# Halving the first two blocks of the first token tile, and a new order of the front, in a gated linear attention with a feed-forward network

## The chip, the cores and the metric

The kernel runs on one core of a Trainium2 chip. The metric is device microseconds of one execution. The engines are TensorE (PE, with its weight loads shown apart as PEld), VectorE (DVE), ScalarE (ACT), GpSimd (POOL) and SyncE (SP), which here only issues transfers.

## The reference

An mLSTM attention over 4 sequences, 8 heads, 768 steps and head size 40 gives `y`. The 3072 tokens of 320 features then go through a feed-forward layer of 2048 hidden features:

```python
C = f_stab * C + i_stab * outer(vt, kt)          # per head, 40 x 40
n = f_stab * n + i_stab * kt
y[t] = sigmoid(o_gate[t]) * (C @ qt) / max(|n . qt|, 1)

h = x @ w_in
g = where(h >= 1, h, where(h <= -1, 0, (h + 1)**2 / 4))
out = g @ w_out
```

All inputs and the output are float32.

## The kernel before

**Attention.** The 768 steps are cut into 6 chunks of 128, so that there are 24 units `n` (chunk `n // 4`, sequence `n % 4`), each of 8 heads by 128 steps. For a unit, `score.n` multiplies keys by queries on PE and the decay matrix `A` onto that on DVE; `main.n` multiplies with the values on PE (`up`), adds the carried state from chunk 1 on, divides on DVE and POOL (`z`, `y`, with the sigmoid of the output gates `sig`), transposes the result on PE, copies its high part to `xh` on ACT and writes the low part to `xl` on DVE. `carry.n` makes the state for the next chunk.

**Feed-forward.** A tile `j` of 512 tokens is four units, `X[j] = (xh, xl)`. The hidden features are 16 blocks of 128 columns; block number `x` is `16 * j + fc`. `mm.x` (function `mm1`, line 833) is eight PE matmuls of 512 columns into one PSUM bank; `relu.x` is two ACT instructions, `max.x` one DVE instruction. The second product comes in two forms. `out.x` takes the float32 result `r` and the float32 weights `of`: eight matmul records a block. The split form makes a high part (`gh.x`, ACT) and a low part (`gl.x`, DVE), and multiplies with split weights `oh`, `ol`: `outh.x` and `outl.x`, twelve matmuls a block. Before, blocks 0 to 9 use `out`, blocks 10 to 95 the split form. The split weights of block pair `i` are made by `so.i` (one ACT, one DVE instruction).

**Weights.** `W.k` loads a packed part of the weights: even `k` is 256 columns of `w_in` (768 KB), odd `k` 256 rows of `w_out` (640 KB). `w.k` steps convert it. For an even `k` they are, in order: `mg` and `lo` on ACT, `and` and `or` on DVE, `wh` on ACT, `wl` on DVE. An odd `k` has the first four. All of it lies beside the attention of chunks 0 and 1 and the first tile.

**Gates of the first chunk.** `fi.0` loads them, `sums.0` runs their scans on DVE, `mask` and `add` build the exponents of a sequence on PE, and `dec` takes the exponential on ACT. `bmax`, `bsum`, `btail` do the same scans for chunks 1 to 4 at once; between the first two, SP sends the running maxima through memory (`m_b`, four small transfers). `og.c` loads the output gates of chunk `c` (640 KB), `sig.c` takes their sigmoid on ACT. `hot.k` are `k` matmuls of zeros, which do no work.

**Order.** The order of everything is written out by hand in the string `STEPS` (lines 48 to 161). `InOrder` (line 174) makes each engine run its instructions in that order, SP its transfers too. So an instruction that waits holds up all that follow it on its engine. Up to eight transfers of SP's queue are under way at a time.

The steps around the change, as they are before: `og.0` is the 21st transfer of SP, `W.0` the fourth; `mm.0` comes after all four `main.n` of chunk 0 have been transposed, since `mm1` needs all 512 tokens of `X[0]`:

```python
    def load_og(c):
        t = sig[c] = ld.tile([P, B, DM], F32, name="sig", bufs=1)
        nc.sync.dma_start(t.rearrange("p b e -> p (b e)"), og[c, :, :B * DM])
```

Of the kernel before, what the change touches and what calls it, by code (L numbers as in the profile page):

```python
# [19 lines left out]
L = 128  # L20
NC = S // L
DM = H * D
# [179 lines left out]
def mlstm_ffn_kernel(ctx, tc, qk, qs, qn, vk, og, fi0, fi, fib, w_in, w_out, cst, out):  # L202
# [362 lines left out]
    def load_og(c):  # L565
        t = sig[c] = ld.tile([P, B, DM], F32, name="sig", bufs=1)
        nc.sync.dma_start(t.rearrange("p b e -> p (b e)"), og[c, :, :B * DM])

    def sigmoid(c):
        nc.scalar.activation(sig[c], sig[c], AF.Sigmoid)  # L570
# [292 lines left out]
    def mm2(x, g, part, ts=range(NTC)):  # L863
        j, fc = divmod(x, NFC)
        if j not in ops:
            ops[j] = [psum_a() for _ in range(NTC)]
# [165 lines left out]
```

## Time and profile before

| | us |
|---|---|
| median of 3 runs | 467.97 (467.7 to 468.16) |
| the profiled execution | 469.77 |
| its span, first to last instruction | 467.8 |
| PE busy | 459.0 (98%) |
| DVE busy | 353.6 (76%) |
| ACT busy | 326.0 (70%) |
| POOL busy | 145.2 (31%) |

The span is what the trace shows; 1.97 us of the profiled execution lie outside it. In the timeline, PE matmuls overlap one another, so what one costs is the distance from its start to the start of the next, and a row with `xN` merges N of them.

### The profile page before, as it was taken

Reading aid. Unit: us, or ns where it says so; the run is one execution under the profiler, and the core shown is the slowest. Engines: PE = TensorE matmul, PEld = TensorE weight load, DVE = VectorE, ACT = ScalarE, POOL = GpSimd, SP = SyncE. Lnnn points to the kernel's source line nnn. Section 1 sums busy time; section 2 is a strip of 40 time slices with the busy share of each in tenths; the row PEclk is TensorE's granted clock in tenths of the full one; section 3 lists DMA queues with packets and bytes.
Section 4 is the critical chain, followed back from the end, with each engine's and each line's share of the span. In section 5 each row is a group of like instructions: output and inputs, shape, how many; then the busy total and the mean of one; then the engine's idle time right before and its main releaser. Section 6 shows DMA issues by size and latency. Waiting matters only on the chain.

```text
span 467.8 us, 8748 instructions
## 1 busy us (share of the span) xinstructions
PE 459.0 (98%) x3312; PEld 407.8 (87%) x3312; DVE 353.6 (76%) x635; ACT 326.0 (70%) x587; POOL 145.2 (31%) x153
## 2 busy tenths in 40 slices
PE   6999999999999999999999999999999999999997
PEld 3788787888989999989999989989989898889896
DVE  5686879689999899998988889877876676243443
ACT  3659889989887677858576878757768564555562
POOL 2364123132353454542334445253113232000000
PEclk9899999999999999999999999999999999999999
DMA  6898956916084445564337353362482000000001
GB/s 204 287 299 275 351 142 227 349 45 168 28 232 121 110 139 156 141 179 112 104 106 196 80 170 90 71 189 53 118 240 80 2 0 1 2 28 29 0 1 56
DMA packets 23048, 60.60 MB, mean 130 GB/s; under 512 B 2599, under 2 KB 9535, under 8 KB 23007
## 3 DMA queue, kind: packets, MB, share of 16 engines
q1 hardware_dynamic: 22719, 59.81, 43.0%
q8 instruction: 26, 0.43, 0.4%
q10 hardware_dynamic: 288, 0.25, 0.2%
q14 instruction: 15, 0.12, 0.1%
HBM read 55.96 MB, written 4.01 MB: 128 GB/s over the span
## 4 chain that ended last, share of the span: by engine, by line
PE 96%; DMA 1%; SPq 1%; issue 1%; ACT 0%; DVE 0%; DVEq 0%
PE ps L188 96%; DMA raw<-in_qk 1%; SPq L188 1%; ACT mg L188 0%; ACT xh L188 0%; DVE z L188 0%; ACT r L188 0%; SPq L185 0%; DVE y L188 0%; DVEq L188 0%; DVE ow L188 0%
## 5 line engine op out<-in xcount | busy, mean ns | idle before, releaser
L188 PE MATMUL ps<-oh,gh 128*128 128x320 f32 x344 | 104.7, 314 | 0.0
L188 PE MATMUL ps<-ow,gh 128*128 128x320 f32 x344 | 102.9, 309 | 0.0
L188 PE MATMUL ps<-xh,wh 128*128 128x512 f32 x288 | 101.4, 406 | 0.9 <-ACT xh L188 0.9
L188 PE MATMUL ps<-xh,wl 128*128 128x512 f32 x288 | 98.2, 395 | 0.0
L188 ACT ACTIVATE r<-ps,half 128x512 f32<-128x512 f32 x96 | 65.4, 682 | 44.3 <-PE ps L188 38.1
L188 DVE SCALAR_TENSOR_TENSOR r<-ps,r 128x512 f32<-128x512 f32 x96 | 64.9, 686 | 35.1 <-ACT r L188 34.8
L188 DVE TENSOR_TENSOR gl<-r,gh 128x512 fp32r<-128x512 f32 x86 | 65.6, 772 | 22.3 <-ACT gh L188 21.4
L188 ACT CAST gh<-r 128x512 fp32r<-128x512 f32 x86 | 52.5, 615 | 40.7 <-PE ps L188 25.9
L188 PEld LDWEIGHTS ps<-ow,gh 128*128 128x128 f32 x344 | 64.7, 188 | 1.4
L188 PEld LDWEIGHTS ps<-oh,gh 128*128 128x128 f32 x344 | 64.6, 188 | 1.4
L188 PE MATMUL ps<-oh,gl 128*128 128x320 f32 x344 | 65.6, 311 | 0.0
L188 PEld LDWEIGHTS ps<-xh,wl 128*128 128x128 f32 x288 | 54.0, 188 | 12.9
L188 ACT ACTIVATE r<-r 128x512 f32<-128x512 f32 x96 | 60.7, 633 | 3.0
L188 PE MATMUL ps<-xl,wh 128*128 128x512 f32 x192 | 60.3, 395 | 0.0
L188 PEld LDWEIGHTS ps<-xh,wh 128*128 128x128 f32 x288 | 50.3, 188 | 8.7 <-ACT xh L188 1.1
L188 PEld LDWEIGHTS ps<-oh,gl 128*128 128x128 f32 x344 | 54.3, 188 | 1.1
L188 ACT ACTIVATE Abc<-Abc,nA 128x128 f32<-128x128 f32 x160 | 50.1, 392 | 3.6 <-POOL Abc L188 3.5
L188 POOL TENSOR_TENSOR v<-vk,G 128x328 f32<-128x328 f32 x36 | 29.1, 811 | 67.5 <-issue 26.2
L188 POOL TENSOR_TENSOR m<-m 128x1024 bf16<-128x1024 f32 x16 | 32.1, 2009 | 48.1 <-DVE m L188 43.0
L188 PEld LDWEIGHTS ps<-xl,wh 128*128 128x128 f32 x192 | 36.0, 188 | 8.8
L188 DVE SCALAR_TENSOR_TENSOR stk<-raw,ident,qs 120x1024 fp32r<-120x1024 f32 x28 | 39.3, 1405 | 4.8 <-ACT raw L188 4.8
L188 POOL TENSOR_TENSOR y<-y,z 128x320 f32<-128x320 f32 x24 | 20.0, 834 | 68.9 <-DVE y L188 68.9
(145 smaller groups left out, 699.2 us busy)
## 6 DMA issues: line engine op xcount, KB each, us to landing
qs<-in_qs SPq DMA_DIRECT2D x28, 480.0 KB
Abc<-a_d SPq DMA_DIRECT2D x20, 512.0 KB
vk<-in_vk SPq DMA_DIRECT2D x20, 324.0 KB
wraw<-in_w_in SPq DMA_DIRECT2D x8, 768.0 KB
wraw<-in_w_out SPq DMA_DIRECT2D x8, 640.0 KB
sig<-in_og SPq DMA_DIRECT2D x6, 640.0 KB
qn<-in_qn SPq DMA_DIRECT2D x20, 180.0 KB
raw<-in_qk SPq DMA_DIRECT2D x20, 160.0 KB
```

The source lines that it names most:

```text
L188: r = getattr(self.engine, name)(*args, **kwargs)
```

## The change

Four things are changed, all of them in how the work is cut and ordered; what is computed is the same.

1. The first two blocks of the first tile (`fc` 0 and 1 of tile 0) are made in two halves of 256 tokens. `am.fc.h` is `mm1` for half `h` alone (eight matmuls of 256 columns), `ar` and `ax` are its `relu` and `max`, `ao` its second product for two of the four token groups. The results lie in tiles of the pool `ow`.
2. `X[j]` is laid out by halves: `[half][k][256]` in place of `[k][512]`. A whole block's matmul now reads its 512 columns in two runs of 256.
3. The output gates of chunk 0 come in two transfers of 320 KB (`og.0.0`, `og.0.1`), with a sigmoid for each (`sig.0.0`, `sig.0.1`).
4. `STEPS` is new from start to end. Blocks 6 to 9 take the split form (four `gh`, four `gl` and their `outh` and `outl` in place of `out.6` to `out.9`). The other steps are the same in number, in another order. The `hot` matmuls are 20 before and 20 after.

The new front, cut after the first use of the second product:

```
fi.0 mask.0 og.0.0 id.0 sums.0 hot.4 sig.0.0 add.0 dec.0.0 dec.0.1 fb.0 bmax.0 hot.2 mask.2 add.2 mask.1
add.1 dec.1.0 gtail.0 gex.0 qk.0 score.0 score.0 score.0 qk.1 score.1 score.1 vv.0 one.0 v1.0 dec.1.1
vv.2 bmax.0 bsum.0 bsum.0 dec.2.0 dec.2.1 v1.2 W.0 mask.3 w.0 w.0 main.0 qk.3 W.1 v1.1 score.1 main.1
add.3 dec.3.1 dec.3.0 hot.2 hot.2 bsum.0 btail.0 btail.0 btail.0 score.3 main.0 main.0 w.0 hot.2 hot.2
hot.2 hot.2 main.1 hot.2 w.0 w.0 main.1 w.1 w.1 btail.0 main.1 score.3 score.3 qk.2 w.0 main.0 main.0
exps.0 score.2 main.0 v.1 v2.1 carry.1 main.1 v.0 v2.0 score.2 score.2 v1.3 main.2 og.0.1 main.1 sig.0.1
w.1 main.3 v.4 am.0.0 w.1 main.2 main.2 main.2 main.3 decs.0 main.2 main.3 main.3 W.2 carry.0 v2.4 w.2
main.2 main.3 main.3 decs.0 w.2 w.2 w.2 cs.0 A.6 prep.6 prep.6 carry.1 am.1.0 carry.0 am.0.1 ar.0.0
ax.0.0 ar.0.1 ax.0.1 am.1.1 qn.5 w.2 w.2 v.5 v2.5 carry.4 main.5 -- ar.1.0 ax.1.0 qn.4 main.4 carry.5
carry.5 carry.5 ao.0.0 ...
```

The diff of the code:

```diff
+    def load_og(c, part=None):
+        if not part:
+            sig[c] = ld.tile([P, B, DM], F32, name="sig", bufs=1)
+        bs = slice(0, B) if part is None else slice(2 * part, 2 * part + 2)
+        nc.sync.dma_start(sig[c][:, bs].rearrange("p b e -> p (b e)"), og[c, :, bs.start * DM:bs.stop * DM])
...
+    def halves(x):
+        return x.rearrange("p k t -> p (k t)").rearrange("p (h k t) -> p h k t", h=2, t=TT // 2)
...
-        xh, xl = X[j]
-        cs = slice(r * L, (r + 1) * L)
+        xh, xl = (halves(x)[:, r // 2] for x in X[j])
+        cs = slice(r % 2 * L, (r % 2 + 1) * L)
...
-    def mm1(j, fc):
-        xh, xl = X[j]
+    def mm1(j, fc, hs=slice(0, 2)):
+        xh, xl = (halves(x)[:, hs] for x in X[j])
...
-        hp = psum_a()[:, :TT]
+        hp = psum_a()[:, :(hs.stop - hs.start) * TT // 2]
...
-            nc.tensor.matmul(hp, w[:, wi, fs], x[:, xi, :], start=(i == 0), stop=(i == len(prod) - 1))
+            nc.tensor.matmul(hp, w[:, wi, fs], x[:, :, xi, :], start=(i == 0), stop=(i == len(prod) - 1))
...
+    def scratch(x, hh):
+        if x not in early:
+            early[x] = ow.tile([P, 656], F32, name="ow")
+        return early[x][:, hh * TT // 2:(hh + 1) * TT // 2]
...
+        if kind == "am":
+            block[n, ns[1]] = mm1(0, n, slice(ns[1], ns[1] + 1))
+        elif kind == "ar":
+            gs[n, ns[1]] = relu(block[n, ns[1]], scratch(*ns))
+        elif kind == "ax":
+            largest(block[n, ns[1]], gs[n, ns[1]])
+        elif kind == "ao":
+            mm2(n, gs[n, ns[1]], "r", range(2 * ns[1], 2 * ns[1] + 2), 2 * ns[1])
```

## Rows read from the trace of the kernel before

**Rows 1.** The page, sections 1 and 2: PE, and PE's granted clock in 40 slices.

```profile
PE 459.0 (98%) x3312; PEld 407.8 (87%) x3312; DVE 353.6 (76%) x635; ACT 326.0 (70%) x587; POOL 145.2 (31%) x153
...
PEclk9899999999999999999999999999999999999999
```

**Rows 2.** The chain that ended last: start us, us, what.

```profile
34.55 338.67 PE ps L188 x2487
...
373.22 91.13 PE ps L188 x588
```

**Rows 3.** Busy time by stretch: us, then PE, PEld, DVE, ACT, POOL, PEclk, DMA.

```profile
0.00:34.55 34.55, 29.24 (x237) 22.11 (x238) 23.62 (x70) 17.35 (x28) 14.08 (x29) 0.95 0.85 263
34.55:118.00 83.45, 83.45 (x492) 69.54 (x493) 68.16 (x119) 75.08 (x136) 25.18 (x26) 1.00 0.68 220
```

**Rows 4.** The timeline of PE, 0 to 35 us: start us, us, operation, idle before.

```profile
2.56 1.49 PE L188 MATMUL ps<-late_t,idb 128*128 128x512 bf16 x3
3.84 1.06 PE L188 MATMUL ps<-zeros 128*128 128x512 bf16 x2
...
5.57 0.39 PE L188 MATMUL ps<-ac,pick 96*128 96x128 bf16 x4 [0.18 <-DVE ac L188]
...
6.45 0.59 PE L188 MATMUL ps<-zeros 128*128 128x512 bf16 x2
...
19.47 2.06 PE L188 MATMUL ps<-raw 40*128 40x128 f32 x32
21.46 1.04 PE L188 MATMUL ps<-zeros 128*128 128x512 bf16 x4
...
24.91 1.88 PE L188 MATMUL ps<-ow,Abc 128*128 128x41 f32 x16
...
29.52 0.85 PE L188 MATMUL ps<-ident,y 128*128 128x128 f32 x6
...
31.83 0.87 PE L188 MATMUL ps<-ow 128*120 128x123 f32 x6
```

**Rows 5.** The timeline of PE at a block, two unsplit second products and a split one.

```profile
36.52 0.63 PE L188 MATMUL ps<-xh,wh 128*128 128x512 f32 x2
...
38.38 0.79 PE L188 MATMUL ps<-C,qn 120*128 120x123 f32 x6
...
71.80 4.47 PE L188 MATMUL ps<-ow,r 128*128 128x320 f32 x16
76.11 0.80 PE L188 MATMUL ps<-C,qn 120*128 120x123 f32 x6
...
404.10 0.75 PE L188 MATMUL ps<-oh,gl 128*128 128x320 f32 x4
...
405.85 0.75 PE L188 MATMUL ps<-oh,gl 128*128 128x320 f32 x4
```

**Rows 6.** The timeline of DVE, 11 to 36 us.

```profile
15.49 0.62 DVE L188 TENSOR_TENSOR fi_b<-fi_b,m_b 128x128 f32<-128x128 f32 x2 [2.22 <-DMA m_b<-m_r]
...
16.66 0.42 DVE L188 TENSOR_TENSOR_SCAN fi_r<-rst,fi_r 128x128 f32<-128x128 f32 x1
...
18.05 1.28 DVE L188 TENSOR_TENSOR Abc<-ps,Abc 128x512 f32<-128x512 f32 x2
```

**Rows 7.** The timeline of ACT: the first weights landed, and the first block's activation.

```profile
7.37 0.89 ACT L185 ACTIVATE mg<-wraw 128x768 f32<-128x768 f32 x1 [5.36 <-DMA wraw<-in_w_in]
8.17 1.05 ACT L188 ACTIVATE win<-wraw 128x768 uint16<-128x768 uint16 x1
...
37.73 0.70 ACT L188 ACTIVATE r<-ps,half 128x512 f32<-128x512 f32 x1
```

**Rows 8.** Groups of ACT over the whole run: count, busy us, mean ns, idle before.

```profile
L188 ACT CAST gh<-r 128x512 fp32r<-128x512 f32 x86 | 52.5, 615 | 40.7 <-PE ps L188 25.9 <-DVE r L188 14.6
```

**Rows 9.** What ACT waited for, 34.55 to 118 us: total, times, longest.

```profile
ACT mg L188 <- DVE ow L188: 2.2, 3, 1.3
...
ACT wh L188 <- DVE win L188: 1.8, 1, 1.8
```

More of the change, by code (lines that the diff above doesn't have):

```diff
@@ L563, in row, with sigmoid @@
         return n % B * NC + n // B
[L565 to L570, printed above, removed]
+    def load_og(c, part=None):
[3 more added lines that the diff above has]
+        nc.sync.dma_start(sig[c][:, bs].rearrange("p b e -> p (b e)"), og[c, :, bs.start * DM:bs.stop * DM])
+    def sigmoid(c, part=None):
+        x = sig[c] if part is None else sig[c][:, 2 * part:2 * part + 2]
+        nc.scalar.activation(x, x, AF.Sigmoid)
     def load_qk(n):
@@ L809, in main @@
         j, r = divmod(n, NTC)
-        if r == 0:
+        if j not in X:
             X[j] = (xs.tile([P, 3, TT], F32R, name="xh"), xs.tile([P, 2, TT], F32R, name="xl"))
-        xh, xl = X[j]
-        cs = slice(r * L, (r + 1) * L)
+        xh, xl = (halves(x)[:, r // 2] for x in X[j])
+        cs = slice(r % 2 * L, (r % 2 + 1) * L)
         xv = xp[:, :3 * P].rearrange("p (k t) -> p k t", t=L)
@@ L839, in mm1, with relu @@
         for i, (w, wi, x, xi) in enumerate(prod):
-            nc.tensor.matmul(hp, w[:, wi, fs], x[:, xi, :], start=(i == 0), stop=(i == len(prod) - 1))
+            nc.tensor.matmul(hp, w[:, wi, fs], x[:, :, xi, :], start=(i == 0), stop=(i == len(prod) - 1))
         return hp
-    def relu(hp):
-        r = mo.tile([P, TT], F32, name="r", bufs=4)
+    def relu(hp, r=None):
+        if r is None:
+            r = mo.tile([P, TT], F32, name="r", bufs=4)
         nc.scalar.activation(r, hp, AF.Relu, bias=half, scale=0.5)
@@ L861, in low, with mm2 @@
         return gl
-    def mm2(x, g, part, ts=range(NTC)):
+    def mm2(x, g, part, ts=range(NTC), t0=0):
         j, fc = divmod(x, NFC)
-        if j not in ops:
-            ops[j] = [psum_a() for _ in range(NTC)]
+        for t in ts:
+            if (j, t) not in ops:
+                ops[j, t] = psum_a()
         i, k = divmod(fc, 2)
@@ L871, in mm2 @@
                 rhs = y[:, fc, :] if y is oh else y[i][:, k, :]
-                nc.tensor.matmul(ops[j][t][:, :DM], g[:, t * L:(t + 1) * L], rhs,
+                nc.tensor.matmul(ops[j, t][:, :DM], g[:, (t - t0) * L:(t - t0 + 1) * L], rhs,
                                  start=(fc == 0 and n == 0 and part != "gl"), stop=(fc == NFC - 1 and part != "gh"))
@@ L883, in store @@
         if both or t % 2 == 0:
-            nc.vector.tensor_copy(o[:, :cut], ops[j][t][:, :cut])
+            nc.vector.tensor_copy(o[:, :cut], ops[j, t][:, :cut])
         if both or t % 2:
             sl = slice(cut, DM) if both else slice(0, DM)
-            nc.scalar.copy(o[:, sl], ops[j][t][:, sl])
+            nc.scalar.copy(o[:, sl], ops[j, t][:, sl])
         if both:
@@ L892, in store @@
             (nc.scalar if t % 2 and j == NC - 1 else nc.sync).dma_start(to, o)
+    early = {}
+    def scratch(x, hh):
+        if x not in early:
+            early[x] = ow.tile([P, 656], F32, name="ow")
+        return early[x][:, hh * TT // 2:(hh + 1) * TT // 2]
     NG = B * S // TT * NFC
@@ L934, in mlstm_ffn_kernel @@
         n = ns[0]
-        if kind == "mm":
+        if kind == "am":
[6 more added lines that the diff above has]
+            mm2(n, gs[n, ns[1]], "r", range(2 * ns[1], 2 * ns[1] + 2), 2 * ns[1])
+        elif kind == "mm":
             block[n] = mm1(*divmod(n, NFC))
```

226 rows, old and new, of the table STEPS are left out of this document.

## The prediction

> **What bounds the kernel now.** I read the page first. PE is busy for 98% of the span, and its granted clock is below full in the first two slices alone [rows 1]. The chain of work that ended last says the same in order of time: from 34.55 us, the first `mm`, it is PE without a break, but for a hundredth of a microsecond at 373.22, up to 464.35 [rows 2]. So there are two places where time can be won: PE's work after 34.55, whatever shortens it, and the 34.55 us ahead, in which PE shows 29.24 us busy, but with twenty `hot` matmuls among it and gaps [rows 3]. Then I read the stretch right behind. From 34.55 to 118 PE is busy throughout, and ACT for 75.08 of 83.45 us, DVE for 68.16 [rows 3]: there the weights are converted, and ACT has 8.37 us to spare. After 118 nothing but PE is near its limit. Last I took prices: of PE by the distance of starts [rows 4, 5], of DVE and ACT from their timelines and groups [rows 6 to 8].
>
> **Blocks 6 to 9 split.** Two unsplit second products take 76.11 - 71.80 = 4.31 us, so 2.155 each; a split one takes 405.85 - 404.10 = 1.75 [rows 5]. Four of them save 4 x 0.405 = 1.6 us of PE, all after 34.55, where PE is the chain. What is added is four `gh` of 0.615 us [rows 8], 2.5 us of ACT, and four `gl` on DVE, both in the stretch where ACT is busiest. They cost nothing only as long as ACT's spare time covers them (below).
>
> **The halves.** An `am` is eight matmuls of 256 columns. No row shows that size in this type. Below it lie the pairs of 123 columns at 0.104 us ((0.79 - 0.27) / 5 for six `C,qn`, 0.27 being the last one's length), above it the 320 columns at 0.146 [rows 5]. I take 0.119, nearer the lower one: 0.95 us an `am`, 3.8 for all four against 3.72 for two whole blocks of 38.38 - 36.52 = 1.86 [rows 5]. The ends are -0.4 and +1.0 us. ACT runs eight instructions in place of four: between 0 and 4 x 0.7 us more [rows 7], and I take half, 1.3. `ao` is `out` in two pieces at the same price.
>
> **The front.** Four legs, each by the queue that sets it.
>
> Leg 1, PE to the first scores. `add.0` waits for `sums.0`, whose place on DVE is unchanged, so it starts at 5.57 as now [rows 4]; masks and `hot.4` fit before. Then in order, at full clock: `add` 0.88 (6.45 - 5.57), two `hot` 0.44 (0.22 each by four in 1.04), `mask.2` 0.44, `add.2` 0.88, `mask.1` 0.44, `add.1` 0.88, a transpose 0.12, sixteen `score` matmuls of 0.06 and their tail 1.2 [rows 4]: 5.57 + 5.28 = 10.85. The data must be there by 9.65: `qk.0` ends the first 1069 KB of SP's queue (96 + 320 + 77 + 256 + 320), and now 1120 KB (96 + 256 + 768) land by 7.37 [rows 7]. That holds.
>
> Leg 2, DVE. Three score products of 0.60 (18.05, two in 1.28), a copy of 0.15, `bsum` 16.66 - 15.49 = 1.17, the fourth product 0.60 [rows 6]: 10.9 + 3.7 = 14.6. Here `bsum` waits for `m_b`, as it does now (2.22 us of idle ahead of it [rows 6]); the four transfers are asked for at 8 to 10 us with the 656 KB of `vv` ahead of them, and DVE comes for them at 12.85. Behind that wait stand `score.1`'s second product and `main.1` on PE.
>
> Leg 3, PE from `main.1`. At 14.7: `up` 16 x 0.11 = 1.8, `add.3` 0.88, four `hot` 0.88, `score.3` 1.0, ten `hot` 2.2, six transposes 0.7, four more 0.45, `score.2` 1.0 [rows 4]: 14.7 + 8.9 = 23.6. DVE has about 8.4 us in the same time, and is close.
>
> Leg 4, PE to the end of the second block. `score.2`'s two products on DVE, 1.3 with the tail: 24.9. Two `up` 3.6, `am.0.0` 0.95, transposes 0.33, `decs` 0.6, transposes 0.33, `carry.0` 0.71 (31.83 to 32.54 [rows 4]), three `am` 2.85: 24.9 + 9.4 = 34.3.
>
> Now the same work, both blocks included, ends at 38.38 [rows 5]. **The front gains 4.0 us.** In it the halves do one thing: `am.0.0` and `am.1.0` run while units 2 and 3 are still divided and transposed. The first sigmoid, on half the gates, runs while PE and DVE are at the first sums; the second one and its two table loads lie beside `main.2` and `main.3` on PE, and are 1.6 us early for the first product that needs it. The extra transfer is one more issue on SP, covered.
>
> [...]
>
> **The stretch of ACT.** PE comes 4.0 us earlier. ACT doesn't: now its first `relu` starts at 37.73 [rows 7], with both halves of `prep.4` done; then the first `ar` starts at about 33.8 with only one half of `prep.6` done, which is 1.2 us less work. So ACT leads by 2.7. From there it has 75.08 + 2.5 + 1.3 = 78.9 us to do, while PE needs 83.45 - 1.6 = 81.85 less the 1.3 of lead: 80.5. Its spare time falls from 8.37 to 1.6 us. Adding up both lists from the last `am` on, an estimate by the same prices, each `mm` finds its weights 0.7 to 1.5 us early: the tightest, `mm.10`, falls at 33.4 + 46.3 = 79.7 on PE, and its `wh` ends after 40.3 us of ACT's work from 35.4, with 1.5 of waits for transfers at 77.2, `wl` on DVE behind it by 79.0. So the cover nearly holds: I take 1.0 us of stalls, between 0 and the 6.8 by which the spare time falls.
>
> **Sum.** -1.6 - 4.0 + 1.0 = -4.6 us. The profiled execution is 469.77 with a span of 467.8; it lies 1.8 above the median of the runs, a difference that I leave as it is: 465.2 for a profiled execution, **463.4** for the median 467.97.
>
> **Rivals.**
>
> *ACT becomes the bound.* Its waits for DVE inside the weight conversions are 2.2 + 1.8 = 4.0 us now [rows 9], and the rest of the 8.37 are waits for PE. For it: spare time of 1.6. Against: the new order puts two or three ACT instructions between `lo` and `wh`, which is what DVE needs. If the 4.0 come back, PE stalls 2.4; if the others do too, 6.8. The middle gives 467.97 - 5.6 + 4.5 = 466.9.
>
> *The front isn't won.* `W.0` moves from SP's fourth place to behind `m_b`, which waits for a scan that ends at 7.9; so it is asked for at about 10.2, not 2.56. It took 4.8 us to 7.37 [rows 7]: landing at 15.0, converted far enough (0.8 + 1.05 [rows 7]) at 16.9, and DVE comes to `and` at 17.4. Behind `and` stand `main.1`'s division and all that follows. The ten `hot` cover 1.1 us more. From a landing at 16.6 each microsecond costs one; at 19.6 the time is 467.97 - 4.6 + 3.0 = 466.4.
>
> *The layout of x slows every whole block (slower).* 94 whole blocks make 752 matmuls that read their 512 columns in two runs. [...] Against it: the mask matmuls read a 128-column tile four times over, four runs, at 0.45 us a piece, and the zeros, one run, at 0.47 [rows 4]. [...]
>
> **How the numbers follow.** Forecast 0.52. No stalls and a front a little better, 461.5: 0.07. ACT as bound 0.20, of which 0.11 ends faster, 0.06 the same, 0.03 slower, by where between 2.4 and 6.8 the stall falls and whether another cost comes with it. The front not won 0.13: 0.06, 0.05, 0.02. The layout 0.08, slower. A difference under 0.2% is about what a measurement of this kernel can't tell from none; with that, faster 0.52 + 0.07 + 0.11 + 0.06 = 0.76, same 0.11, slower 0.08 + 0.03 + 0.02 = 0.13. The range for 8 in 10 takes in the rivals on the fast side: 461.2 to 467.8.
>
> **What the new profile would show.** `am.1.1` ends near 34.3, the first `am` starts near 28.6; `mg` on the first weights starts near 15.0; eight starts of a whole block are still 1.86 apart; the unsplit second products number 48 records, not 80; ACT is busy for over 96% of the 80 us behind the front, and PE has gaps there of about 1 us in all. I am wrong if the first scores come after 11, if DVE waits for weights between 16 and 20, or if PE shows gaps of more than 3 us between 40 and 110.

## The result, and the profile after

The changed kernel takes 470.76 us (median of 10, 469.38 to 473.15), the kernel before 467.92 in the same runs (10, 467.45 to 470.04). The ratio is 1.0061 with an interval of 1.0040 to 1.0083: **slower by 0.6%**, where 463.4 was forecast. The profiled execution of the changed kernel is 472.88 with a span of 471.1. The single executions of the changed kernel fall into groups by the clock, as will be seen.

The page of the changed kernel: sums by engine, PE's granted clock in 40 slices, and the chain that ended last by engine.

```profile
PE 462.3 (98%) x3343; PEld 411.9 (87%) x3344; DVE 357.0 (76%) x641; ACT 331.5 (70%) x597; POOL 158.1 (34%) x153
...
PEclk9979999999999999999999999999999999999999
...
PE 88%; DVE 9%; issue 1%; ACT 1%; DMA 0%; DVEq 0%
```

Where the kernel before had PE alone in the chain from 34.55 on [rows 2], 9% of the chain is now DVE. And the low slice of the clock has moved from the second to the third [rows 1].

Busy time by stretch (us, then PE, PEld, DVE, ACT, POOL, PE's granted clock as a share of full speed, DMA), for [rows 3], and with it the stretches around the low clock:

```profile
0.00:34.55 34.55, 31.20 (x235) 24.07 (x237) 24.05 (x69) 18.97 (x29) 13.52 (x28) 0.93 0.88 268
34.55:118.00 83.45, 82.76 (x519) 70.39 (x518) 72.90 (x125) 76.60 (x139) 26.65 (x27) 0.99 0.67 212
...
22.60:29.70 7.10, 6.67 (x65) 6.19 (x63) 6.86 (x15) 5.96 (x10) 2.64 (x3) 1.00 1.02 333
29.70:36.50 6.80, 6.80 (x34) 6.80 (x34) 3.28 (x11) 3.55 (x8) 3.18 (x4) 0.50 1.04 328
```

From 29.7 to 36.5, in the middle of the first two blocks, PE's granted clock was 0.50. In the 7.1 us ahead it had been busy for 6.67, with products of 41, 123 and 128 columns; the product behind the last `hot` started at 22.55.

PE's timeline where the legs of the forecast begin and end (start, us, what; a matmul costs the distance to the next start):

```profile
8.95 0.54 PE L190 MATMUL ps<-ac,pick 96*128 96x128 bf16 x4
...
11.51 2.06 PE L190 MATMUL ps<-raw 40*128 40x128 f32 x32
...
29.77 0.78 PE L190 MATMUL ps<-xh,wh 128*128 128x256 f32 x2
...
38.49 0.28 PE L190 MATMUL ps<-xh,wl 128*128 128x256 f32 x1
38.61 0.80 PE L190 MATMUL ps<-v,vk 128*120 128x123 f32 x6
39.24 0.50 PE L190 MATMUL ps<-C,qn 120*128 120x123 f32 x3
```

The first scores start at 11.51 (forecast 9.65), the first `am` at 29.77 (28.6), and the second block ends at 38.61 (34.3; before 38.38 [rows 5]). Behind it stands `v,vk`, a product of `carry`, 0.63 us. The kernel before makes it *ahead* of its second block: counted by kind, and the `hot` and the blocks themselves aside, the PE matmuls up to there are the same in both but for these six. The like moment in the changed kernel is therefore 39.24.

The largest waits of PE behind that, with what ended them:

```profile
48.87 0.81 PE L190 MATMUL ps<-ow 128*128 128x320 f32 x2 [0.22 <-DVE Abc L190]
...
102.78 0.42 PE L190 MATMUL ps<-ow,gh 128*128 128x320 f32 x1 [0.40 <-DVE ow L190]
...
135.49 0.74 PE L190 MATMUL ps<-xh,wh 128*128 128x512 f32 x2 [0.25 <-DVE hv L190]
...
253.81 0.30 PE L190 MATMUL ps<-ident,ex 128*128 128x128 f32 x1 [1.10 <-DVE ex L190]
```

All four were ended by DVE. They add up to 2 us; what is lost in smaller pieces doesn't show one by one, so the accounts below split each span at the end of the second block (`v,vk` included). A gain or a loss in the **front** is one of that moment, one in the **rest** is one of PE's work or PE's waits behind it.

| profiled execution | front ends | rest | span |
|---|---|---|---|
| before | 38.38 | 429.4 | 467.8 |
| forecast | 34.3 | 428.8 | 463.2 |
| changed | 39.24 | 431.9 | 471.1 |

The front is 4.9 us later than forecast and the rest 3.1 longer.

### The profile page after: what moved, and what is told of

It reads as the page before. It is cut to its first block, busy times and chain, and to the rows that moved or that the text cites. A ratio compares the mean times of both kernels' runs of the same rounds, so it can differ in the third digit from the quotient of the medians.

```text
span 471.1 us, 8846 instructions
## 1 busy us (share of the span) xinstructions
PE 462.3 (98%) x3343; PEld 411.9 (87%) x3344; DVE 357.0 (76%) x641; ACT 331.5 (70%) x597; POOL 158.1 (34%) x153
## 4 chain that ended last, share of the span: by engine, by line
PE 88%; DVE 9%; issue 1%; ACT 1%; DMA 0%; DVEq 0%
PE ps L190 88%; DVE gl L190 1%; DVE Abc L190 1%; DVE ow L190 1%; DVE stk L190 1%; DVE hv L190 1%; DVE r L190 1%; DVE wl L190 0%; ACT Abc L190 0%; DVE z L190 0%; DMA fi<-in_fi 0%; DVE win L190 0%; DVE C L190 0%; DVE fi_b L190 0%; DVE y L190 0%
## 5 line engine op out<-in xcount | busy, mean ns | idle before, releaser
L190 PE MATMUL ps<-oh,gh 128*128 128x320 f32 x360 | 109.7, 315 | 0.0
L190 PE MATMUL ps<-ow,gh 128*128 128x320 f32 x360 | 107.7, 309 | 0.4 <-DVE ow L190 0.4
L190 PE MATMUL ps<-xh,wh 128*128 128x512 f32 (+1 forms) x294 | 102.8, 404 | 0.2 <-DVE hv L190 0.2
L190 PE MATMUL ps<-xh,wl 128*128 128x512 f32 (+1 forms) x294 | 99.5, 393 | 0.0
L190 DVE TENSOR_TENSOR gl<-r,gh 128x512 fp32r<-128x512 f32 x90 | 70.5, 790 | 24.3 <-ACT gh L190 22.7
L190 PEld LDWEIGHTS ps<-ow,gh 128*128 128x128 f32 x360 | 67.8, 188 | 1.8 <-DVE ow L190 0.7
L190 PE MATMUL ps<-oh,gl 128*128 128x320 f32 x360 | 68.8, 311 | 0.0
L190 PEld LDWEIGHTS ps<-oh,gh 128*128 128x128 f32 x360 | 67.7, 188 | 1.2
L190 PE MATMUL ps<-xl,wh 128*128 128x512 f32 (+1 forms) x196 | 61.1, 393 | 0.0
L190 POOL TENSOR_TENSOR v<-vk,G 128x328 f32<-128x328 f32 x36 | 33.0, 919 | 49.1 <-PE ps L190 31.6
L190 POOL TENSOR_TENSOR m<-m 128x1024 bf16<-128x1024 f32 x16 | 34.3, 2146 | 33.9 <-DVE m L190 31.1
```

The source lines that it names most:

```text
L190: r = getattr(self.engine, name)(*args, **kwargs)
```

## The experiments

The kernels of one group below ran on one chip with their own runs of the kernel before: 468.33 for the first four, 467.95 for the next four, 468.05 for the three after that, 467.94 for the last. The ratio with its interval is the recorded one, which isn't exactly the quotient of the two medians.

### The `hot` matmuls spread

Theory: the clock, granted at 0.50 from 29.7 to 36.5, fell since PE had nothing but small matmuls from 22.6 on; with the `hot` spread it stays full, and the time is 468.6. Rival: the clock takes little, the order's waits do.

```diff
 dec.3.0 hot.2 hot.2 bsum.0 btail.0 btail.0 btail.0 score.3 main.0 main.0 w.0 hot.2 hot.2
-hot.2 hot.2 main.1 hot.2 w.0 w.0 main.1 ...
+main.1 w.0 w.0 main.1 ...
-v.1 v2.1 carry.1 main.1 v.0 v2.0 score.2 score.2 v1.3 main.2 og.0.1 main.1 sig.0.1 w.1 main.3 v.4 am.0.0
+v.1 v2.1 carry.1 hot.2 main.1 v.0 v2.0 score.2 score.2 v1.3 main.2 hot.2 og.0.1 main.1 sig.0.1 w.1 main.3 hot.2 v.4 am.0.0
```

> The changed kernel, with three of the five `hot.2` that stand together after `score.3` moved apart: one after `carry.1`, one after `up` of unit 2, one after `up` of unit 3. Still 20 `hot` matmuls. [...] Theory B, VectorE and ScalarE set the middle of the kernel whatever the front does: the front ends sooner, PE's gaps between 40 and 130 us grow by as much, and the time stays at 470.8.

Measured: 470.82 (ratio 1.0036, 1.0014 to 1.0058). The stretch that was slow, in the run's profile, and where the fourth leg begins and ends:

```profile
29.70:36.50 6.80, 6.80 (x61) 6.66 (x61) 4.29 (x12) 4.43 (x11) 3.18 (x4) 1.00 1.05 325
...
30.38 0.59 PE L190 MATMUL ps<-xh,wh 128*128 128x256 f32 x2
...
36.22 0.79 PE L190 MATMUL ps<-v,vk 128*120 128x123 f32 x6
```

The granted clock stayed at 1.00 there. From the first `am` to the end of the second block it took 36.22 - 30.38 = 5.84 us, where the changed kernel took 8.84 and the forecast was 5.7. So the low clock cost 3.0 us in the profiled execution. The median hardly moved all the same, and the mean granted clock of each execution says why. A stretch of 6.8 us at 0.50 puts the mean over 470 us at 0.993 (1 - 3.4 / 470; the low start isn't in it: the run with three moves, below, has a mean of 1.0 with starts of 512 columns 0.43 us apart up to 10.66). Five of the changed kernel's ten executions have 0.999 or more, so they don't hold that stretch, and they take 469.38 to 470.85 already. In this run eight of twelve have 0.998 or more (468.87 to 471.28), and four have 0.988 to 0.995. So the spread `hot` didn't keep every execution at the full clock, nor was the fall what the median lost. The rest is 431.9, to the tenth that of the changed kernel; what was lost there isn't the clock's. That the fall came of the small matmuls, as the theory has it, isn't shown: the run with three moves, below, speaks against it.

### Blocks 6 to 9 unsplit in the new order

```diff
-gh.6 ... gl.6 ... outh.6.2.3 outh.6.0.1 outl.6
+out.6          (and 7, 8, 9 likewise)
```

> The changed kernel, with blocks 6 to 9 back in the unsplit form in their places: 1.6 us more of PE, four `gh` (2.1 to 2.5 us of ScalarE) and four `gl` (2.4 us of VectorE) less. Theory A, the split overloads ScalarE and VectorE in the middle, where the changed kernel has 4.2 us more of PE stalls than the kernel before: the stalls fall by 3, time 469.4. Theory B, the stalls come from the order and not from the added work: they stay, and the time is 470.8 + 1.6 = 472.4.

Measured: 474.54 (1.0113, 1.0084 to 1.0142). The front is the same (256 columns start 0.21 us apart from 30.15 to 36.55 and 0.12 apart behind it, the profile's mean clock is 0.993), the rest 434.6: 2.7 longer, the 1.6 of the split and 1.1 more. Four of the six executions have a mean clock of 0.992 or 0.993; the two at 1.0 take 472.43 and 473.20, near theory B's 472.4. Of the four large waits three are still there, `ex` with 1.1 us among them, and two of 0.4 us behind `r` and `v` are new. So they don't come from the added `gh` and `gl`, and in this order the split is worth more than its price. (`so.3` and `so.4` keep their early places, so nothing is said of those.)

### The split alone, in the old order

```diff
-... out.6 ... out.7 ... gh.11 ... gl.11 ... out.8 so.5 mm.13 out.9
+gh.6 so.3 so.3 gl.6 ... outh.6.2.3 outh.6.0.1 outl.6 ... gh.7 so.4 so.4 gl.7 ... outh.7.2.3 outh.7.0.1 outl.7
+... gh.11 ... gl.11 ... max.10 gh.8 gl.8 ... outh.8.2.3 outh.8.0.1 outl.8 gh.9 gl.9 so.5 mm.13 outh.9.2.3 ...
```

> The kernel before, with only blocks 6 to 9 put into the split form (and `so.3`, `so.4` moved ahead of them). Theory A, the spare time of ScalarE covers the added 2.5 us: 467.9 - 1.6 = 466.3. Theory B, the split is paid back as stalls of PE behind ScalarE or VectorE: 467.9 or above.

Measured: 473.44 (1.0099, 1.0068 to 1.0131). One wait alone took twice the 1.6 us, 3.38 us for `gh.8`, and the clock was low behind it (three `oh,gl` take 1.17 us from 96.16 on, where four take 0.75 at 89.98; the profile's mean clock is 0.996):

```profile
94.74 0.41 PE L189 MATMUL ps<-oh,gh 128*128 128x320 f32 x1 [3.38 <-ACT gh L189]
```

`gh.8` stood on ACT behind the conversion of `W.13` and `relu.10`. That is a fault of where I put it, and says nothing yet of the split; the run was made again with another place (below).

### The new front, then the old order

The changed kernel up to `am.1.1` with the spread `hot`, all that is left in the order of the kernel before, blocks 6 to 9 unsplit.

> The front of the first run here (new front with the `hot` spread) up to `am.1.1`, and from there the order of the kernel before, with blocks 0 and 1 in halves and blocks 6 to 9 unsplit. Theory A, the front wins about 2 us once the clock holds and the stalls behind it belong to the new order of the middle: 467.9 - 2.0 = 465.9. Theory B, ScalarE comes no earlier than now, so PE that is ahead only waits later: 467.9.

Measured: 470.39 (1.0036, 1.0020 to 1.0052), above both theories. The profile shows three things.

```profile
5.59 0.39 PE L189 MATMUL ps<-ac,pick 96*128 96x128 bf16 x4 [0.69 <-DVE ac L189]
...
40.90 0.73 PE L189 MATMUL ps<-xh,wh 128*128 128x512 f32 x2 [0.40 <-ACT wh L189]
41.89 0.74 PE L189 MATMUL ps<-xh,wl 128*128 128x512 f32 x2 [0.27 <-DVE wl L189]
...
15.10:21.90 6.80, 6.53 (x35) 4.79 (x38) 5.57 (x18) 4.94 (x7) 1.73 (x2) 0.50 0.99 281
```

First, in this execution the early sums ran at the full pace (starts 0.22 apart from 5.59 on; 0.43 in the changed kernel up to 8.95), and the first scores came at 9.76: leg 1 was sized right, for the full clock. Second, the clock fell at another place, to 0.50 from 15.1 to 21.9, with the same steps up to there as in the run with the spread `hot` alone; the spread doesn't hold it. Third, PE, early at the third block, waited for its weights, `wh` from ACT and `wl` from DVE, and 0.45 us for the carry ahead of it. Behind 42 us PE's waits are as few as in the kernel before. With the front at 37.72 and a rest of 430.5 nothing of the new front's gain is left, and the waits at 102, 135 and 252 belong to the new order. Nor is the low stretch the whole reason for the median: ten of the twelve executions here have a mean clock of 0.996 or more and take 469.54 to 471.13. Where these lose their time no trace here shows.

### Three late steps moved

```diff
-relu.13 main.8 w.14 outh.9.2.3 qn.10 gh.11 outh.9.0.1 so.5 w.14
+relu.13 main.8 so.5 w.14 outh.9.2.3 qn.10 gh.11 outh.9.0.1 w.14
-relu.18 gl.16 main.8 v.10 mm.21 main.9 main.10 relu.20 max.18
+relu.18 main.8 v.10 mm.21 main.9 main.10 relu.20 max.18 gl.16
-g5.5 main.14 mm.46 main.16
+main.14 mm.46 g5.5 main.16
```

> The changed kernel with three steps moved, each at a place where PE stood still in its trace: the last gate step of chunk 5 (product ex on DVE at 252.74, PE waiting 1.26 us) goes behind the block mm.46; gl.16 (2.38 us on DVE at 132.64 while GpSimd ran m, PE losing 0.41) goes behind max.18; the DVE half of so.5 (101.90, PE losing 0.67) goes ahead of a weight conversion. Theory A, each stall is a fault of its own place in the order: 1.26 + 0.41 + 0.67 = 2.3 us less than the changed kernel, 468.4, and DVE ex, gl and ow no longer release PE there. Theory B, DVE is behind PE as a whole and the next step is late instead: no more than 0.7 us less, 470.1 or above, with new stalls within 5 us of the old ones.

Measured: 470.62 (1.0061, 1.0034 to 1.0089), with a rest of 430.8, 1.1 less than in the changed kernel, not 2.3. By place: the waits at 135 and 102 are no longer among the large ones, and the one at 252 has moved. PE no longer waits for `ex`, but loses 1.2 us between 250 and 260 to the steps behind it. So neither theory holds for all of them.

The same profile settles something of the clock. Up to `am.1.1` the steps and the `hot` are those of the changed kernel, and after a low start (0.43 us apart up to 10.66) the granted clock stayed at 1.00 through the stretch of small products:

```profile
22.00:29.70 7.70, 7.21 (x63) 5.95 (x62) 7.56 (x14) 7.48 (x12) 3.64 (x4) 1.00 1.02 343
29.70:36.50 6.80, 6.77 (x60) 6.67 (x60) 4.91 (x15) 4.21 (x10) 3.19 (x4) 1.00 1.04 326
```

So this order of small matmuls doesn't have to bring the fall, and the front doesn't need the spread `hot` to be without it. Six of the twelve executions here have a mean clock of 1.0 (468.75 to 470.16), the six others 0.988 to 0.993 (471.07 to 474.77).

What was behind the wait at 135 is plain. Ahead of the move, DVE and GpSimd:

```profile
131.91 3.11 DVE L190 TENSOR_TENSOR gl<-r,gh 128x512 fp32r<-128x512 f32 x2
134.94 0.49 DVE L190 TENSOR_TENSOR hv<-ps,G 128x328 f32<-128x328 f32 x1
...
132.13 2.34 POOL L190 TENSOR_TENSOR m<-m 128x1024 bf16<-128x1024 f32 x1
```

and behind it, in the next run, which has the same moves:

```profile
128.79 0.49 DVE L190 TENSOR_TENSOR hv<-ps,G 128x328 f32<-128x328 f32 x1
...
131.32 0.68 DVE L190 TENSOR_TENSOR gl<-r,gh 128x512 fp32r<-128x512 f32 x1
...
128.28 2.34 POOL L190 TENSOR_TENSOR m<-m 128x1024 bf16<-128x1024 f32 x1
```

The second `gl`, `gl.16`, started beside GpSimd's `m` and ended 0.55 us after it: the two take 3.11 us, where `gl.16`, moved from beside `m`, takes 0.68. `hv` takes 0.49 us beside `m` behind the move, as it did ahead of the move without `m`.

### The moves and the `hot` together

```diff
-fi.0 mask.0 og.0.0 id.0 sums.0 hot.4 sig.0.0
+fi.0 mask.0 og.0.0 id.0 sums.0 hot.6 sig.0.0
```

and the edits of the first and the last run.

> The three moves and, on top, three of the five bunched hot.2 spread over the last divisions as in the run with the spread alone, and hot.6 in place of hot.4 ahead of the first sums. Theory A (places, and a clock that falls when PE has only small matmuls): full clock from about 5 us on and through 29 to 37, the second block of the first tile ends near 35, time 466.9 to 467.6, below the kernel before. Theory B (given back): not under 468.5.

Measured: 468.63 (1.0016, 0.9997 to 1.0034), 2.1 less than the changed kernel but on theory B's side of the two. The six `hot` close the gap ahead of the sums, PE is at the full pace from 7.3 on (starts of 512 columns 0.22 apart, 0.43 ahead of it; from 10.3 on in the first run), the first scores come at 10.57, and the second block ends at 35.18, front 35.86. The rest is 430.9. At 250 to 260 the step that I had moved, `g5`, was now itself in the way, on ACT:

```profile
250.96 0.28 ACT L190 ACTIVATE G<-ps 128x128 f32<-128x128 f32 x1 [1.54 <-PE ps L190]
251.13 0.19 ACT L190 ACTIVATE nA<-ps 128x32 f32<-128x32 f32 x1
251.21 0.48 ACT L190 CAST xh<-ps 128x384 fp32r<-128x384 f32 x1
```

ACT waits for the transpose of `ex`, which PE makes behind `mm.46`, and `xh`, on which DVE and then PE depend, stands behind that wait.

### The kernel before with more `hot`

```diff
-dec.1.1 dec.0.0 score.1
+dec.1.1 dec.0.0 hot.6 score.1
```

> The kernel before with six more matmuls of zeros ahead of its first scores, where PE waits 1.65 us for a load. Theory A, the profiled execution of the kernel before holds 1.7 us of a low clock at 11.7 to 15.1 us that its faster executions do not have, so the 38.38 us at which its first two blocks end overstates what a new front can win: with the zeros the clock stays full there, the two blocks end at 36.6 to 36.9, and all executions lie near 468.0. Rival, the lower clock costs nothing there because PE waits for loads and for DVE anyway: the two blocks end at 38.2 or later and the time is within 0.3 us of the median of the kernel before in the same runs or above it.

Measured: 468.11 (0.9997, 0.9979 to 1.0016). In its profile the starts of 512 columns are 0.22 apart from 7.25 on and the granted clock is 1.00 in every stretch up to 60, and the second block ends at 36.40. The next run settles it better, since it has the order of the kernel before untouched.

### The layout alone

```diff
-        xh, xl = X[j]
+        xh, xl = (halves(x) for x in X[j])
...
-            nc.tensor.matmul(hp, w[:, wi, fs], x[:, xi, :], ...)
+            nc.tensor.matmul(hp, w[:, wi, fs], x[:, :, xi, :], ...)
```

> The kernel before with nothing but the x tiles laid out by halves, so that every whole block reads its 512 columns in two runs. Theory A, two runs cost what one costs: starts 0.23 us apart, time within 0.3 us of the kernel before. [...]

Measured: 468.12 (1.0004, 0.9981 to 1.0028). Two runs cost what one costs: the busy time of the groups of PE, by their mean, is that of the kernel before.

```profile
L188 PE MATMUL ps<-xl,wh 128*128 128x512 f32 x192 | 60.3, 395 | 0.0
```

(the same line, with 60.3 and 395, stands in the groups of the kernel before). And the end of the second block, in an execution of 468.13:

```profile
36.38 0.39 PE L188 MATMUL ps<-xh,wl 128*128 128x512 f32 x1
36.62 0.79 PE L188 MATMUL ps<-C,qn 120*128 120x123 f32 x6
...
11.70:15.10 3.40, 3.35 (x32) 2.22 (x33) 2.10 (x6) 1.65 (x4) 1.13 (x2) 1.00 0.70 188
```

From 11.7 to 15.1 the profiled execution of the kernel before has a granted clock of 0.50:

```profile
11.70:15.10 3.40, 3.40 (x14) 1.67 (x13) 1.57 (x3) 0.28 (x1) 1.13 (x2) 0.50 0.64 172
```

Here the clock is full (1.00), and the second block ends at 36.62 in place of 38.38. The rest is 429.6, as before. So the profiled 469.77 holds 1.76 us that the median execution of 467.97 doesn't. The executions of the kernel before agree: beside the last run below, the 13 of 17 with a mean clock of 0.999 or more take 467.50 to 468.29, the four with 0.996 or less 469.28 to 469.77.

### The split alone, placed again

```diff
-gh.6 so.3 so.3 gl.6 mm.8 w.9 main.7 A.8 ... main.7 w.10 w.10 main.5 w.10 relu.9
+gh.6 so.3 mm.8 w.9 main.7 A.8 ... main.7 w.10 w.10 main.5 w.10 so.3 gl.6 relu.9
-w.12 w.12 gh.11 v2.7 w.13 ... w.13 gl.11 ... max.10 gh.8 gl.8 ... outl.8 gh.9 gl.9
+w.12 w.12 gh.8 v2.7 w.13 ... w.13 gl.8 ... max.10 gh.9 gl.9 ... outl.8 gh.11 gl.11
```

> The kernel before with blocks 6 to 9 split, as in the run of the split alone, but the two places changed at which PE stood still there: gh.8 and gl.8 take the place of gh.11 and gl.11, which nobody needs yet, gh.9 and gl.9 that of gh.8 and gl.8, and the DVE half of so.3 and gl.6 come after the division of unit 7 in place of ahead of it. Theory A, the split is worth its 4 x 0.405 = 1.6 us of PE as soon as every high part is ready in time: 466.3 to 466.7, without the 3.55 us of waiting at 91. Theory B, ACT and DVE have no room in that stretch and the wait moves on: not under 467.6.

Measured: 468.38 (1.0008, 0.9988 to 1.0027): no difference. The large wait is gone, but the rest is 430.0 against 429.6. The 1.6 us that the split saves are waited off in pieces between 80 and 110, of which the largest is

```profile
102.70 0.55 PE L189 MATMUL ps<-ident,y 128*128 128x128 f32 x3 [0.49 <-POOL y L189]
```

In that stretch DVE is busy for 73.17 us of 34.55 to 118, against 68.16 [rows 3], ACT for 76.56 against 75.08. Theory B, then, for the old order.

### The halves alone, in the old order

```diff
-W.4 mm.0 carry.1 decs.0 prep.4 prep.4 w.2 -- relu.0 w.2 mm.1
+W.4 am.0.0 am.1.0 am.0.1 carry.1 decs.0 prep.4 prep.4 w.2 -- ar.0.0 ar.0.1 w.2 am.1.1
```

(and `ar`, `ax`, `ao` for `relu.1`, `max.0`, `max.1`, `out.0`, `out.1`)

> The kernel before in its own order with nothing but the halves: the first two blocks are made as am.0.0, am.1.0, am.0.1, am.1.1 (the first two do not wait for the last two units), their relu and max in halves too, x laid out by halves. Theory A, the halves fill the wait of 0.89 us that PE has ahead of the first block: 0.9 us less, 467.1. Theory B, what PE wins ahead of the third block it loses waiting there, since the weights of that block are converted on ACT and DVE no earlier (with the new front ahead of the old order PE waited 0.40 for wh and 0.27 for wl at 40.9 to 41.9): 467.7 to 468.2, and a wait of 0.6 us or more ahead of mm.2.

Measured: 471.70 (1.0070, 1.0042 to 1.0097). The wait of the kernel before,

```profile
34.55 0.73 PE L188 MATMUL ps<-xh,wh 128*128 128x512 f32 x2 [0.89 <-ACT xh L188]
```

is filled, and the second block ends at 37.51 with a low clock (0.75 from 10 to 15, 0.93 from 15 to 22), to be set against 38.38 with the like low clock (0.67 and 0.99): 0.87 us, as theory A says. But then

```profile
42.39 0.90 PE L189 MATMUL ps<-C,qn 120*128 120x123 f32 x6 [3.00 <-DVE ow L189]
```

PE waits 3.0 us for a maximum of the halves (`ow` is their buffer), and the clock is low behind it (512 columns start 0.43 apart up to 46.36 and 0.23 apart from 46.72 on; 0.93 from 36.5 to 60). The four halves hold four PSUM tiles where two blocks held two, and the `ar` of the last two stand on ACT behind `wh` and `oh`. Neither theory had this wait; what it tells is that the halves need their `ar` and `ax` at once, as the new order has them.

### Halves and split together

Both edits in one kernel.

> Both of the last two together in the old order: the halves and the split of blocks 6 to 9, no new order. Theory A for both: 468.0 - 0.9 - 1.6 = 465.5. Halves given back, split kept: 466.4. Both given back: 467.6 or more. If it is under 467.4, the new order is what costs the changed kernel its time, and not its parts.

Measured: 472.90 (1.0099, 1.0073 to 1.0125), with the same wait of 3.0 us. It can't tell whether the parts are sound without the new order, since the placing of the halves decides it.

### The gate step once more

```diff
-main.14 mm.46 g5.5 main.16 main.14 max.45 stack.16 main.14
+main.14 mm.46 main.16 main.14 max.45 stack.16 g5.5 main.14
```

> The version with the three moves and the spread zeros, with one step moved once more: the last gate step of chunk 5 stands not right behind mm.46 but behind the copy of unit 16 to xh and the first half of stack.16. Where it stood in the last version ACT waited 1.54 us for its transpose ahead of that copy, DVE then 1.43 us for the copy, and PE lost 1.16 us between 250 and 260 us. Theory A, that is again a fault of one place: no wait of ACT there, PE loses under 0.3 us between 250 and 260, and the time is 467.4 to 467.7. Theory B, the stall moves on a second time: 468.3 or more, PE loses 0.8 us or more between 250 and 262.

Measured: 468.17 (1.0019, 0.9994 to 1.0044). Theory A in the profile: an execution of 467.45 with a span of 465.7, the front at 35.8 and the rest at 429.9, 1.0 less than in the version before it; between 250 and 260 PE loses 0.13 us. The median is higher: four of the twelve executions lie above 470, with a lower mean clock (0.989 to 0.993), and none of the 17 of the kernel before in these runs. So it can't be told from the kernel before, and no version here beats it.

## Why the prediction was wrong

| profiled execution | front ends | rest | span |
|---|---|---|---|
| before | 38.38 | 429.4 | 467.8 |
| before's order, clock full (layout alone) | 36.62 | 429.6 | 466.2 |
| changed | 39.24 | 431.9 | 471.1 |
| `hot` spread | 36.89 | 431.9 | 468.8 |
| three moves | 37.30 | 430.8 | 468.1 |
| moves and `hot` | 35.86 | 430.9 | 466.8 |
| gate step later | 35.8 | 429.9 | 465.7 |
| split alone, placed again | 36.51 | 430.0 | 466.5 |

The forecast of 463.4 lies 7.4 us below the median, and the executions with and without the low clock have to be told apart. The five of the ten with a mean clock of 0.999 or more have a median of 470.49. For these the steps below, with leg 1 as in the profiled execution, add up to 463.4 + 3.1 (stalls behind the front beyond the 1.0 that I took) + 1.8 (the base) + 1.2 (leg 1) + 0.63 (`v,vk`) = 470.1. The three with 0.992, the profiled one among them, take 472.88 to 473.15; there the fall of the clock comes on top.

**The clock** was the step that failed in the fourth leg of the profiled execution, whose prices are those of the full clock. It fell to 0.50 from 29.7 to 36.5: PE was busy for 6.67 of the 7.10 us ahead of it, with no gap over 0.43. It cost 3.1 us in the fourth leg (8.84 in place of 5.7; 5.84 where the clock was full). The stretch, 6.80 us, was twice as long as the one of the kernel before, 3.40. But the median doesn't hold it, and what makes it come is open: the same front with the same `hot` ran without it in the run with three moves, and with the `hot` spread it came at another place. I had also read [rows 1] as two slices below full; the first digit is a 9 like all others, and only the second slice is lower.

**Leg 1** assumed "at full clock" as well. Full, the first scores come at 9.76 against the 9.65 of the forecast; in the changed kernel the starts are 0.43 us apart up to 8.95, and the scores come at 11.51. In the old order low starts (layout alone: 0.42 apart up to 6.41) cost nothing, since PE waits for the load of its first scores anyway (1.27 us there); in the new one PE itself is the chain. In the kernel before that wait is

```profile
9.59 0.46 PE L188 MATMUL ps<-raw 40*128 40x128 f32 x2 [1.65 <-DMA raw<-in_qk]
```

Of the 1.86 us, 1.2 are left at the first `am`. Legs 2 and 3 held (13.3 us from the first scores to the end of `score.2` at 24.82; the forecast had 13.95), and so did the landing of `W.0`: `mg` starts at 15.15 for 15.0, so the rival by which the front isn't won through `W.0` is out.

**"The same work, both blocks included"** was wrong by one product: 0.63 us of `v,vk` lie behind the second block now. These three, 3.1 + 1.2 + 0.63, are the 4.9 us of the profiled front.

**The base.** "A difference that I leave as it is": the 1.8 us between the profiled execution and the median was the low stretch at 11.7, and most executions don't have it (13 of the 17 beside the last run). The front was measured against 38.38 when the median's is at 36.6. So even with the forecast's front of 34.3, plus `v,vk`, the median could have gained only 36.62 - 34.93 = 1.7, not 4.0.

**The split** was priced right as far as the runs show: the records without split weights number 48, and unsplit the rest is 2.7 us longer, which holds the 1.6. **"The stretch of ACT"** was mis-sized, and it is the largest of the terms that the median holds: 431.9 - 429.4 + 1.6 = 4.1 us of stalls behind the front, where I took 1.0. The row that I trusted, ACT's spare time, was the wrong one. ACT is busy for 76.60 us, 92% of the stretch, not over 96%, and the waits of PE end on DVE, whose 72.90 us look roomier still. A sum over 83 us says how much fits in, not when each piece is due. I also left out that the split needs `so.3` and `so.4` early: their DVE halves start at 79.19 and 96.36, 61 and 57 us ahead of where they were (the first two lines here are of the changed kernel, the others of the kernel before):

```profile
79.19 0.82 DVE L190 TENSOR_TENSOR ow<-ow,oh 128x640 fp32r<-128x640 f32 x1
96.36 0.81 DVE L190 TENSOR_TENSOR ow<-ow,oh 128x640 fp32r<-128x640 f32 x1
...
139.77 0.79 DVE L188 TENSOR_TENSOR ow<-ow,oh 128x640 fp32r<-128x640 f32 x1
152.88 0.82 DVE L188 TENSOR_TENSOR ow<-ow,oh 128x640 fp32r<-128x640 f32 x1
```

That the order decides was shown by moving steps: three moves and a fourth took 2.0 of the 4.1 us out, with the work unchanged. For the other 2.1, between 36 and 120 us, no run here names one cause; the split alone in the old order meets 2.0 us of such waits there too.

**The layout** is free (1.0004, 0.9981 to 1.0028): the 192 matmuls of `xl,wh` take 395 ns on average, their columns in one piece or in two. That rival is out.

Of what the prediction named as proof against it, one came true, the first scores after 11, and one didn't: DVE waited for no weights between 16 and 20. Gaps of PE of more than 3 us between 40 and 110 depend on the measure. PE is idle for 0.69 us there (busy for 69.31 of 70.00); by the distances of starts it loses 2.4 to 3.3 us more than in the kernel before, an estimate that varies with what is taken as usual for a kind of matmul.

**The output gates in two transfers** weren't tried alone. Their sigmoids and table loads stood where the forecast had them (the second ones at 25.06 to 28.39), and no wait of PE in the front ends on them.

## What to carry to other kernels

Where PE shows 100% in a tuned stretch, the other engines may have been put in place to the microsecond for it: work taken from PE there (the split alone: 1.6 us saved, none gained) is worth nothing until each step that PE meets sooner is ready sooner, so ask of every wait-free meeting how early the other side was, and not of a stretch how much time an engine has left. Compare a forecast's base with the median only after taking the low-clock stretch of the profiled execution out, if the other executions lack it; the mean clock of each execution tells. Do the same with the profile of the result, before the clock is made the cause of a median that half the executions reach without its fall.

## What the runs showed of the hardware

**DVE beside GpSimd.** Of the 90 `gl` (`gl<-r,gh`, 128x512) of the changed kernel, the 48 that no GpSimd instruction overlaps take 0.685 us on average and 0.695 at most; the 42 others 0.909, and up to 2.38 (at 132.64, beside the 2.34 us of `m`). Which of the two starts first parts them: the 17 that start ahead of the GpSimd instruction take 0.68 to 0.69, and of the 25 that start behind it 20 take 0.71 to 2.38 and end 0.54 to 0.55 us after it. Why, no run shows. `hv` (`hv<-ps,G`) ran its 0.49 us beside `m` (at 128.79 in the run with the moves and the `hot`). In the profile such a `gl` looks like a slow DVE instruction, not like a wait (the row at 131.91 above has no idle time), so the list of waits doesn't show it.

**The clock in the first 40 us.** The same steps gave a stretch with a granted clock of 0.50 at 11.7 to 15.1 or none (the old order: kernel before, layout alone), at 29.7 to 36.5 or none (the new front: changed kernel, three moves), and at 15.1 to 21.9 or none (the new front with the `hot` spread: two runs). Each profile is one execution; the mean clock of the others says how often a stretch occurs, not where: 5 of 10 executions of the changed kernel are under 0.999, 4 of 17 of the kernel before beside the last run.

**A half costs what its columns cost.** Eight matmuls of 256 columns in this type start 0.114 us apart at the full clock and 0.213 where it was 0.50 (changed kernel, `am.1.1` and `am.0.0`), next to 0.233 for 512 at the full clock: 0.92 us an `am`, where 0.95 was the estimate.
